# Start of the QKV projection and order of later loads in a fused attention and SwiGLU kernel

## Chip, cores and metric

The kernel runs on one core of a Trainium2 chip. The metric is the time of one execution on the device, in microseconds; lower is better.

## The reference

`x` is 2048 tokens by 576 columns, bfloat16. It is normalized once (`xn`) and goes through two branches, whose results are added to `x`:

```python
xn = _layernorm(x)                                  # (x - mean) / sqrt(var + 1e-5), by token
# A: qkv = xn @ wqkv; 32 heads of 18; each token attends to itself and to the tokens
#    2, 4, ... 14 before it (8 positions, softmax); o @ wo
# B: (silu(xn @ w_gate) * (xn @ w_up)) @ w_down      with 4608 inner columns
return x + _A_ref(xn, A_wqkv, A_wo) + _B_ref(xn, B_w_gate, B_w_up, B_w_down)
```

## The kernel before

Tokens are split into 16 row tiles ("rows" below) of 128 tokens, and four token tiles of four rows each. The order of the work is written out by hand (`tc.manual_schedule()`): each engine runs its instructions in the order in which the Python code issues them. Nearly all transfers are issued from SyncE's queue (SP), in order; each transfer takes the next of eight completion semaphores in turn, and the issue of a transfer waits until the one eight before it has landed. PSUM is a ring of eight banks (`new_ps`, `new_pt`).

**Start, row 0 and row 1** (L477 to L525). The loads at L154 to L165 bring x rows 0 to 3 one by one, the QKV weights in five slices of 128 (the last: 64) input columns, and then x rows 4 to 15 in three transfers. Slice 1 and x row 0 go over ScalarE's queue, all others over SP's. `warm_pe` (L171) runs matmuls on constants until the first data is there. Row 0 is only centred (mean taken off) before it is turned: `ln_stats(0)` takes mean and variance on VectorE by two `bn_stats` (L214) and one `bn_aggr` (L218), `ln_center` (L248) takes the mean off, first for 128 columns and then for the rest, `transp_pe` (L258) turns 128 x 128 blocks on TensorE into PSUM and `copy_pt` (L267) copies them out. Its factor 1/sqrt(var + eps) is multiplied into the products when they leave PSUM (`p_evac`, L363 to L367); `ln_apply(0)` also makes a fully normalized copy, which is turned by a transfer (`transp_dma`). All other rows are normalized fully first (`ln_stats`, `ln_sqrt`, `ln_recip`, `ln_apply`).

The products of row 0 (`p_whole`, L304) go slice by slice: four matmuls of 128 x 432, one for each group of 432 columns of q, k, v, for each slice. Row 1's five blocks are turned between them (L501 to L507): blocks 0 and 1 into the bank of the warm-up (`pt1`), block 2 into `pa`, 3 and 4 into `pb`; `pa` and `pb` held row 0's blocks. ScalarE copies out the first and the last pair, VectorE block 2. Row 1's products of slice 0 follow, then row 0's slice 3 and slice 4 (`p_row0_rest`, two pairs of 64-row halves).

**Rows 1 to 15** (L523 to L577). `p_row` multiplies one row by all weights with 64-row matmuls that run in pairs. Rows 2 to 4 are turned on TensorE inside the products of the row before (`turn`), rows 5 to 15 by transposing transfers (`transp_dma`, L291). Keys and values are stored to the ring tiles `Kr` and `Vr`, or for the later token tiles to a buffer in HBM (`kv_d`, `store`). `load_wd(7)` (L533) loads the eighth chunk of the down projection's weights, 576 KB, after row 1. The tile `wd` holds x and the normalized rows in its first seven chunks until they are used up.

**Token tiles** (L647 to L684). For each token tile nine chunks of 512 inner columns run: `g_pair` (L601) multiplies by the gate and up weights of the chunk, `g_evac` applies silu and the product. The weights of a chunk (1.15 MB, `gu`, four transfers, L182 to L185) stand in one of two slots; those of chunk n + 2 are issued when chunk n is done. In the first token tile, the remaining weights of the down projection (`load_wd`, L193) and of the output projection (`load_wo`, L190) are loaded beside: chunk `ch` issues `load_wd(ch - 1)` for 1 to 7, and chunk 5 also `load_wd(8)`. Attention for the next token tile runs on VectorE in between (a list of pieces that `dve.pump` works off), with its ring loads (`ring_load`, L389). The residual `xr` (four rows of x, two transfers of 288 KB, L672 to L674) is loaded at chunk 0 in the first token tile and at chunk 7 in the others. After chunk 8 the attention output is turned by four transfers (L659), and `d_half` (L630) multiplies by `wd` and `wo` and `d_out` (L642) adds the residual.

Of the kernel before, what the change touches and what calls it, by code (L numbers as in the profile page):

```python
# [70 lines left out]
def kernel(  # L71
# [83 lines left out]
    load_x(nc.sync, 1)  # L155
    load_w(nc.scalar, 1)
    load_w(nc.sync, 0)
    make_identity(nc, ident[:])
# [4 lines left out]
    load_x(nc.sync, 3)  # L163
    for c in range(1, 4):
        nc.sync.dma_start(xc_b[c], x_v[:, 4 * c:4 * c + 4, :])  # L165
    nc.scalar.activation(warm[:], eps_t[:], ACT.Sqrt)

    wp = ps.tile([P, 512], f32, name="warm_ps", tag="ps")
    pt1 = wp[:].bitcast(bf16)

# [35 lines left out]

    sums = {}

    def ln_half(r, k):
# [38 lines left out]
    def ln_center(r, lo=0, hi=D):  # L248
        c, j = divmod(r, 4)
        xc, xn, mv, rstd = ln[c]  # L250
        nc.vector.tensor_scalar(xn[:, j, lo:hi], xc[:, j, lo:hi], mv[:, j, 0:1], None, op0=ALU.subtract)  # L251

    def ln_center_pad(r):
        c, j = divmod(r, 4)
        xc, xn, mv, rstd = ln[c]
        nc.gpsimd.tensor_scalar(xn[:, j, D:DPAD], xc[:, j, 512:D], mv[:, j, 0:1], None, op0=ALU.subtract)

# [218 lines left out]

    warm_pe(10, 1)  # L477
    ln_open(0)
    ln_stats(0)
    ln_center_pad(0)  # L480
    ln_center(0, 0, P)
    ln_sqrt(0)
    pa, pb = new_pt(), new_pt()
# [7 lines left out]
    copy_pt(nc.scalar.copy, 0, (3, 4), pb[:, 2 * P:])  # L491
    ln_recip(0)
    ln_apply(0)
    ln_recip(1)
    ln_apply(1)

    t = [new_ps("qkv_ps") for g in range(NG)]
    p_whole(0, t, 0)
    p_whole(0, t, 1)
    p_whole(0, t, 2, (0, 1))  # L500
    transp_pe(1, (0, 1), pt1)  # L501
    transp_pe(1, (2,), pa)
    copy_pt(nc.scalar.copy, 1, (0, 1), pt1)
    copy_pt(nc.vector.tensor_copy, 1, (2,), pa)
    p_whole(0, t, 2, (2, 3))
    transp_pe(1, (3, 4), pb)
    copy_pt(nc.scalar.copy, 1, (3, 4), pb)  # L507
    u = [None] * NG
# [4 lines left out]
    p_row0_rest(t)  # L513
    ln_stats(2)
    ln_sqrt(2)
    normalize(2)
# [14 lines left out]
    for ring in (Kr, Vr):  # L531
        nc.sync.dma_start(ring[0:1, 0:HALO, :], wz[0:1, :].unsqueeze(1).to_broadcast([1, HALO, D]))
    load_wd(7)  # L533

# [112 lines left out]
    for tt in range(NTT):  # L647
        for ch in range(NCH):
            it = tt * NCH + ch
            for p in range(2):  # L650
                g_pair(tt, ch, p)
                for j in (2 * p, 2 * p + 1):
                    g_evac(ch, j)
                    if it % NCH < NCH - 1 or p == 0:
                        dve.pump(1.4)
            if ch == NCH - 1:
                dve.drain(lambda: chains[0] > tt)
                for r in range(RT * tt, RT * tt + RT):
                    nc.sync.dma_start_transpose(oT[:, :, r * P:(r + 1) * P], QOP[:, r, :])  # L659
            if it + NSLOT < NTT * NCH:  # L660
                load_gu(it + NSLOT)
            if tt == 0:
                if 1 <= ch <= 7:
                    load_wd(ch - 1)
                if ch == 5:
                    load_wd(8)
                for _ in range(3 if ch in (1, 2) else 2):
                    if wo_order:
                        load_wo(wo_order.pop(0))
                if ch == 0:  # L670
                    store(2, 3, 3)
            if ch == (7 if tt else 0):  # L672
                for i in (0, 2):
                    nc.sync.dma_start(xr[:, i:i + 2, :], x_v[:, RT * tt + i:RT * tt + i + 2, :])  # L674
            if ch == 1 and tt < NTT - 1:
                chain(tt + 1)
# [38 lines left out]
```

## Time and profile before

| | us |
|---|---|
| median of 3 runs | 503.55 (503.23 to 503.98) |
| the profiled execution's own time | 504.4 |
| its span | 502.6 |
| TensorE matmul busy | 498.1 |
| VectorE busy | 329.2 |
| ScalarE busy | 200.7 |
| start of the first product of row 0 | 5.93 |
| start of the token tiles (first `g_ps` in the chain) | 59.92 |

PE is TensorE, PEld its weight loads, DVE VectorE, ACT ScalarE, POOL GpSimd, SP SyncE; "SPq" is an issue on SP's queue. A timeline line has the start in us, the length in us, the engine, the line of the kernel, the operation, the tile it writes and reads, the shapes, the count and in brackets the idle time before it. A line of the chain has start, length and what the chain passed through. In the list of waits: who waited for whom, us in total, how often, longest.

### The profile page before, as it was taken

To read this page: it belongs to the slowest core of one execution; us is meant where nothing else is said; L and a number is where in the kernel's file an instruction comes from. 1 tells how busy PE (TensorE), PEld (TensorE's weight loads), DVE (VectorE), ACT (ScalarE), POOL (GpSimd) and SP (SyncE) were. 2 spreads that over 40 slices of the span, in tenths; PEclk is the share of its full clock that TensorE was granted. 3 is DMA by queue.
4 is the path that set the end of the run, shared out by engine and by line. 5 is a ranking of instruction groups with operands and counts; after the bars stand their busy time and mean duration, and the time that the engine had idled before them with its cause. 6 is when DMAs were issued, how large, how long until landed. Compare 5 with 4: busy or idle time off the path is not lost.

```text
span 502.6 us, 13267 instructions
## 1 busy us (share of the span) xinstructions
PE 498.1 (99%) x5795; PEld 333.8 (66%) x5795; DVE 329.2 (65%) x478; ACT 200.7 (40%) x415; POOL 2.6 (1%) x9
## 2 busy tenths in 40 slices
PE   9999999999999999999999999999999999999997
PEld 4555544455899755555999655556999555557997
DVE  6888598888999698999898139995980222221001
ACT  4756657654400155554300454558000454553000
POOL 2000000000000000000000000000000000000000
PEclk9999999999999999999999999999999999999999
DMA  8999989789721036536730054455600335453100
GB/s 316 216 205 230 313 281 312 223 263 305 190 94 61 25 122 206 176 116 222 152 91 37 27 187 139 145 188 154 139 25 14 103 108 181 152 180 38 29 14 25
DMA packets 77186, 75.42 MB, mean 150 GB/s; under 512 B 22708, under 2 KB 72528, under 8 KB 77128
## 3 DMA queue, kind: packets, MB, share of 16 engines
q1 hardware_dynamic: 76840, 73.98, 50.3%
q8 instruction: 45, 0.74, 0.6%
q10 hardware_dynamic: 288, 0.59, 0.3%
q14 instruction: 13, 0.11, 0.1%
HBM read 58.76 MB, written 5.90 MB: 129 GB/s over the span
## 4 chain that ended last, share of the span: by engine, by line
PE 96%; DMA 3%; DVE 0%; ACT 0%; SPq 0%; issue 0%
PE g_ps L601 54%; PE d_ps L630 32%; PE qkv_ps L301 10%; DMA gu<-in_B_w_up_dram 2%; DMA xnT<-wd 1%; DMA wd<-in_A_x_dram 1%; DVE stats L214 0%; DVE wd L251 0%; PE pt L262 0%; ACT ot L644 0%; SPq L182 0%; PE pt L283 0%; DVE mv L218 0%; PE warm_ps L262 0%
## 5 line engine op out<-in xcount | busy, mean ns | idle before, releaser
L601 PE MATMUL g_ps<-xnT,gu 64*128 64x512 bf16 x2592 | 281.5, 376 | 0.3 <-DMA gu<-in_B_w_up_dram 0.3
L601 PEld LDWEIGHTS <-gu 64*128 64x128 bf16 x2592 | 144.8, 94 | 135.6 <-DMA gu<-in_B_w_up_dram 0.8
L630 PE MATMUL d_ps<-wd,hT 64*128 64x288 bf16 x2304 | 152.5, 283 | 0.0
L612 ACT ACTIVATE sg<-g_ps 128x512 bf16<-128x512 f32 x144 | 87.3, 606 | 157.5 <-PE g_ps L601 157.5
L630 PEld LDWEIGHTS <-hT 64*128 64x128 bf16 x2304 | 144.6, 94 | 0.5
L614 DVE TENSOR_TENSOR hT<-sg,uc 128x512 bf16<-128x512 bf16 x144 | 60.0, 418 | 94.3 <-ACT uc L613 94.2
L613 ACT CAST uc<-g_ps 128x512 bf16<-128x512 f32 x144 | 85.2, 592 | 0.0
L414 DVE TENSOR_REDUCE PP<-PP 128x64 f32<-128x1152 bf16 x64 | 84.9, 1345 | 0.4
L301 PE MATMUL qkv_ps<-hT,xnT 64*128 64x432 bf16 (+1 forms) x536 | 50.2, 343 | 0.2 <-DMA xnT<-wd 0.2
L409 DVE TENSOR_TENSOR PP<-QO,Kr 128x2304 bf16<-128x2304 bf16 (+1 forms) x35 | 43.5, 1249 | 7.8 <-DMA Kr<-hT 7.5
L642 DVE TENSOR_TENSOR ot<-d_ps,xr 128x288 bf16<-128x288 f32 x30 | 12.3, 450 | 51.1 <-PE d_ps L630 51.0
L441 DVE TENSOR_TENSOR PP<-Vr,A 128x2304 bf16<-128x2304 bf16 (+1 forms) x35 | 43.2, 1250 | 0.4
L301 PEld LDWEIGHTS <-xnT 64*128 64x128 bf16 (+1 forms) x536 | 25.8, 94 | 22.9 <-DMA xnT<-wd 0.6
L446 DVE TENSOR_TENSOR PP<-PP 128x2304 bf16<-128x2304 bf16 x24 | 32.5, 1353 | 0.3
L630 PE MATMUL d_ps<-wo,xnT 64*128 64x288 bf16 x288 | 29.1, 283 | 0.0
L612 ACT ACT_TABLE_LOAD x5 | 6.4, 1283 | 47.2 <-PE g_ps L601 47.2
L630 PEld LDWEIGHTS <-xnT 64*128 64x128 bf16 x288 | 21.2, 94 | 0.0
L363 ACT CAST hT<-qkv_ps 128x288 bf16<-128x288 f32 (+2 forms) x58 | 21.0, 423 | 0.3 <-DMA kv_d<-hT 0.3
L434 ACT ACTIVATE PP<-PP 128x1024 f32<-128x1024 f32 x4 | 4.2, 1057 | 31.3 <-DVE PP L430 31.2
L644 ACT CAST ot<-d_ps 128x288 bf16<-128x288 f32 x1 | 0.4, 399 | 38.7 <-PE d_ps L630 38.7
L363 ACT CAST QO<-qkv_ps 128x432 bf16<-128x432 f32 (+1 forms) x30 | 12.2, 405 | 7.9 <-PE qkv_ps L301 7.9
L214 DVE BATCH_NORM_STATS2 stats<-wd 128x6 f32<-128x288 bf16 x32 | 12.9, 443 | 3.0 <-DMA wd<-in_A_x_dram 2.8
(53 smaller groups left out, 90.8 us busy)
## 6 DMA issues: line engine op xcount, KB each, us to landing
gu<-in_B_w_gate_dram SPq DMA_DIRECT2D x36, 512.0 KB, 3.8
gu<-in_B_w_up_dram SPq DMA_DIRECT2D x36, 512.0 KB, 5.3
wd<-in_B_w_down_dram SPq DMA_DIRECT2D x9, 576.0 KB, 6.1
kv_d<-hT SPq DMA_DIRECT2D x5, 576.0 KB, 5.9
gu<-in_B_w_gate_dram SPq DMA_DIRECT2D x36, 64.0 KB, 4.8
gu<-in_B_w_up_dram SPq DMA_DIRECT2D x36, 64.0 KB, 4.4
xr<-in_A_x_dram SPq DMA_DIRECT2D x8, 288.0 KB, 5.0
out_dram<-ot SPq DMA_DIRECT2D x16, 144.0 KB, 1.8
```

Source lines behind the costliest of these rows:

```text
L214: nc.vector.bn_stats(sums[r][:, k, :], xc[:, j, k * HALF:(k + 1) * HALF])
L301: return nc.tensor.matmul(t[g][:, 0:G], xT_of(r)[rows, kt, :], w_at(g, kt, rows), start=start, stop=stop)
L363: (nc.vector.tensor_copy if n in dve else nc.scalar.copy)(*parts[n])
L409: nc.vector.tensor_tensor(prod[:, a:b], QO[:, RT * tt + a:RT * tt + b, :], Kr[:, s:s + b - a, :], op=ALU.mult)
L414: nc.vector.tensor_reduce(L[:, w, rs], prod[:, rs].rearrange("p r (h d) -> p r h d", d=DH), axis=AX.X, op=ALU.add)
L441: nc.vector.tensor_tensor(dst[:, a:b], Vr[:, s:s + b - a, :].rearrange("p r (d h) -> p r d h", h=H), A[:, w, a:b].unsqueeze(2).to_broadcas ...
L446: nc.vector.tensor_tensor(dst, acc, pv, op=ALU.add)
L601: mm = nc.tensor.matmul(ring_ps[j][b][:], gu[rows, slot, k, fc], xnT[rows, kt, tok], start=(swap == 0 and kt == 0), stop=(swap == 1 and kt ...
L612: nc.scalar.activation(sg[:], t[0][:], ACT.Silu)
L613: nc.scalar.copy(uc[:], t[1][:])
L614: nc.vector.tensor_tensor(hT[:, ch * FC + j, :], sg[:], uc[:], op=ALU.mult)
L630: mm = nc.tensor.matmul(t[sub][h][:, 0:HALF], a[rows], w[rows, h * HALF:(h + 1) * HALF], start=(swap == 0 and n == 0), stop=(swap == 1 and ...
```

## The change

- The QKV weight slices 0 and 1 are each loaded in two halves of 864 columns; ScalarE's queue takes the upper halves, SP's the lower.
- x rows 8 to 15 come in one transfer.
- Row 0's mean is not taken from `bn_stats`: `ln_mean0` sums x/576 over columns 0 to 287 on ScalarE and over 288 to 575 on VectorE, each with an accumulator output, and `ln_center` takes both sums off. The statistics of row 0 (still wanted for its variance and its normalized copy) move between and behind those of row 1; its square root, reciprocal and apply move behind row 1's copies and row 2's statistics.
- Row 1's blocks 0 to 2 are turned after slice 1's products instead of half way through slice 2's, blocks 3 and 4 after three of slice 2's four; all go to the bank `pb` and are copied by ScalarE.
- One warm-up matmul less.
- `load_wd(7)` leaves the start: chunk 3 issues `load_wd(8)` and chunk 4 `load_wd(7)` beside their own; chunk 5 has one again.
- The store of the last values goes in two parts, not three. The residual `xr` is loaded after chunk 8's output transposes, in all token tiles.

```diff
-    load_w(nc.scalar, 1)
-    load_w(nc.sync, 0)
+    for kt in range(2):
+        for eng, cols in ((nc.scalar, slice(2 * G, 4 * G)), (nc.sync, slice(0, 2 * G))):
+            eng.dma_start(wqkv[:, kt, cols], A_wqkv[kt * P:(kt + 1) * P, cols])
...
-    for c in range(1, 4):
-        nc.sync.dma_start(xc_b[c], x_v[:, 4 * c:4 * c + 4, :])
+    nc.sync.dma_start(xc_b[1], x_v[:, 4:8, :])
+    nc.sync.dma_start(wdf[:, 2 * XC:4 * XC].rearrange("p (r d) -> p r d", d=D), x_v[:, 8:16, :])
...
-    pt1 = wp[:].bitcast(bf16)
...
+    part = const.tile([P, 2], f32, name="part")
+
+    def ln_mean0():
+        xc = ln[0][0]
+        nc.scalar.activation(PP[:, 1, 0:HALF], xc[:, 0, 0:HALF], ACT.Copy, scale=1.0 / D, accum_out=part[:, 0:1])
+        nc.vector.tensor_scalar(PP[:, 1, HALF:D], xc[:, 0, HALF:D], 1.0 / D, None,
+                                op0=ALU.mult, op1=ALU.add, accum_out=part[:, 1:2])
...
-        nc.vector.tensor_scalar(xn[:, j, lo:hi], xc[:, j, lo:hi], mv[:, j, 0:1], None, op0=ALU.subtract)
+        nc.vector.tensor_scalar(xn[:, j, lo:hi], xc[:, j, lo:hi], part[:, 0:1], part[:, 1:2],
+                                op0=ALU.subtract, op1=ALU.subtract)
...
-    warm_pe(10, 1)
+    warm_pe(9, 1)
     ln_open(0)
-    ln_stats(0)
+    ln_mean0()
     ln_center_pad(0)
     ln_center(0, 0, P)
-    ln_sqrt(0)
...
     copy_pt(nc.scalar.copy, 0, (3, 4), pb[:, 2 * P:])
-    ln_recip(0)
-    ln_apply(0)
+    ln_half(0, 0)
     ln_recip(1)
     ln_apply(1)
+    ln_half(0, 1)
+    ln_aggr(0)
...
     p_whole(0, t, 1)
-    p_whole(0, t, 2, (0, 1))
-    transp_pe(1, (0, 1), pt1)
-    transp_pe(1, (2,), pa)
-    copy_pt(nc.scalar.copy, 1, (0, 1), pt1)
-    copy_pt(nc.vector.tensor_copy, 1, (2,), pa)
-    p_whole(0, t, 2, (2, 3))
-    transp_pe(1, (3, 4), pb)
-    copy_pt(nc.scalar.copy, 1, (3, 4), pb)
+    transp_pe(1, (0, 1, 2), pb)
+    copy_pt(nc.scalar.copy, 1, (0,), pb)
+    copy_pt(nc.scalar.copy, 1, (1, 2), pb[:, P:])
+    p_whole(0, t, 2, (0, 1, 2))
+    transp_pe(1, (3, 4), pb[:, 3 * P:])
+    copy_pt(nc.scalar.copy, 1, (3, 4), pb[:, 3 * P:])
+    p_whole(0, t, 2, (3,))
+    ln_sqrt(0)
+    ln_stats(2)
+    ln_sqrt(2)
+    ln_recip(0)
+    ln_apply(0)
...
     p_row0_rest(t)
-    ln_stats(2)
-    ln_sqrt(2)
     normalize(2)
...
-    load_wd(7)
...
                 for r in range(RT * tt, RT * tt + RT):
                     nc.sync.dma_start_transpose(oT[:, :, r * P:(r + 1) * P], QOP[:, r, :])
+                for i in (0, 2):
+                    nc.sync.dma_start(xr[:, i:i + 2, :], x_v[:, RT * tt + i:RT * tt + i + 2, :])
...
-                if ch == 5:
-                    load_wd(8)
+                if ch in (3, 4):
+                    load_wd(11 - ch)
...
                 if ch == 0:
-                    store(2, 3, 3)
-            if ch == (7 if tt else 0):
-                for i in (0, 2):
-                    nc.sync.dma_start(xr[:, i:i + 2, :], x_v[:, RT * tt + i:RT * tt + i + 2, :])
+                    store(2, 3, 2)
```

More of the change, by code (lines that the diff above doesn't have):

```diff
@@ L255, in ln_center_pad @@
         xc, xn, mv, rstd = ln[c]
-        nc.gpsimd.tensor_scalar(xn[:, j, D:DPAD], xc[:, j, 512:D], mv[:, j, 0:1], None, op0=ALU.subtract)
+        nc.gpsimd.tensor_scalar(xn[:, j, D:DPAD], xc[:, j, 512:D], part[:, 0:1], part[:, 1:2],
+                                op0=ALU.subtract, op1=ALU.subtract)
     def transp_pe(r, kts, pt):
```

## The prediction

> **What bounds the kernel now.** I read the share of busy time first, then what TensorE waited for, then the chain that ended last, and then the timeline of the places that these name. The page and TensorE's list of waits:
>
> ```profile
> span 502.6 us, 13267 instructions
> PE 498.1 (99%) x5795; PEld 333.8 (66%) x5795; DVE 329.2 (65%) x478; ACT 200.7 (40%) x415; POOL 2.6 (1%) x9
> ...
> PE warm_ps L174 <- PEq L699: 0.8, 1, 0.8
> PE g_ps L601 <- DMA gu<-in_B_w_up_dram: 0.3, 1, 0.3
> PE qkv_ps L301 <- DMA xnT<-wd: 0.2, 1, 0.2
> ```
>
> TensorE is never without work but for its start and two waits on transfers. Only what shortens the start, or these two waits, or adds a new wait can move the time. The chain places them:
>
> ```profile
> 0.72 3.19 DMA wd<-in_A_x_dram
> ...
> 3.93 0.83 DVE stats L214 x2
> ...
> 18.97 4.60 DMA xnT<-wd
> 23.57 0.05 issue
> 23.62 36.31 PE qkv_ps L301 x396
> ...
> 83.71 7.80 DMA gu<-in_B_w_up_dram
> 91.51 0.05 issue
> 91.56 39.12 PE g_ps L601 x359
> ```
>
> The ends of matmuls are modelled, so I take waits from start to start. At 23.62 a pair comes 0.50 us after the one before it, where 0.18 is usual: row 5's wait costs 0.32. At 91.56 it is 0.71 for 0.21: chunk 4's wait costs 0.50. From 91.56 to the end nothing waits. The timeline of the start:
>
> ```profile
> 5.03 0.56 DVE L251 TENSOR_SCALAR wd<-wd,mv 128x128 bf16<-128x128 bf16 x2
> 5.93 2.00 PE L301 MATMUL qkv_ps<-hT,PP 128*128 128x432 bf16 x10
> 7.16 0.43 DVE L240 TENSOR_SCALAR wd<-wd,mv,rstd 128x576 bf16<-128x576 bf16 x1
> 7.76 0.28 PE L262 MATMUL warm_ps<-ident,wd 128*128 128x128 bf16 x2
> 8.08 0.37 ACT L268 COPY xnT<-warm_ps 128x256 bf16<-128x256 bf16 x1 [0.92 <-PE warm_ps L262]
> 9.24 1.36 PE L301 MATMUL qkv_ps<-hT,PP 128*128 128x432 bf16 x8
> ```
>
> Row 0's centring starts at 5.03, its first product 0.90 later, slice 3's at 9.24, and slice 4's at 10.07 (four products of 0.18 and a 0.1 switch to half rows). Two windows (us, busy time by engine, clock, share of the DMA engines, GB/s):
>
> ```profile
> 3.00:5.50 2.50, 2.40 (x8) 0.68 (x5) 1.50 (x5) 0.44 (x2) 0.40 (x1) 1.00 1.01 401
> 98.00:99.50 1.50, 1.50 (x16) 0.79 (x14) 1.50 (x3) 0.66 (x2) 0.00 (x0) 1.00 0.10 25
> ```
>
> The first window is full: the weights come no faster. By issue and time to landing, slice 3 lands at 2.59 + 6.4 = 9.0 and is used at 9.24; the last of slice 4 lands at 3.92 + 5.9 = 9.8 and its product runs at 10.07. So whatever row 0 gains, TensorE can come forward by some 0.25 us only.
>
> **The change, part by part.**
>
> **Row 0's mean.** Removed ahead of the centring: two statistics and an aggregate, 3.93 to 5.03 = 1.10 us. Added: one half sum on ScalarE and one on VectorE, side by side, and a hand-over. No row shows a summing operation. The nearest are ScalarE's 288-wide ACTIVATE at 0.50 and VectorE's L251 (0.25 for 128 columns, 0.40 for 448, so 0.33 for 288); VectorE took up a ScalarE result 0.04 after its end (9.65 to 9.69). Low bound 0.33 + 0.04, high bound 0.83, the two statistics that go. I take ScalarE's row and 0.1 for hand-over and read-out: 0.60, so centring at 4.53, 0.50 sooner. The Trainium skill's page "VectorE: DVE Perf Modes", section "Two Vector instructions with no wait between them", says that an operation that writes its accumulator out is two instructions, the second a read of it; no row here shows one, and by it (an estimate, with the 0.11 to 0.16 of a one-column RECIPROCAL) VectorE's half is 0.44 to 0.49, still under ScalarE's, so the sum stays.
>
> **Row 1.** From its start the centring needs 2.56 us until row 1 is normalized (7.59). Behind it now: two statistics of row 1, the aggregate, one half statistic of row 0 (0.37 from start to start) in place of a reciprocal and an apply (0.49), reciprocal, apply: 2.5, so 7.03, transposes at 7.1. TensorE ends slice 1's products at 4.53 + 0.90 + 8 x 0.183 = 6.9 and waits 0.2. Then three transposes and three products of slice 2. The next two transposes write the same bank `pb` that ScalarE reads, and so wait for its copies: third transpose's end 0.33 after 7.1, hand-over 0.04, copies 0.27 + 0.37, so 8.1, where the products were done at 7.8: another 0.3 wait, which three banks spared the kernel before. Two transposes 0.11, a product 0.18, four products of row 1 0.73: slice 3 at 9.15 against 9.24. Slice 2 (1.64 + 5.6 = 7.2) is in time.
>
> **Slices in halves.** Two more issues, on two queues, and 0.88 MB in rows half as long. Bounds: nothing, by the window 3.00 to 5.50; or the 267 GB/s of 8.00 to 9.40, where slice 4's equally short rows come, against 401: 0.88 MB in 3.3 us for 2.2, 1.1 more, on all weights behind. I take 0.1: same tensor, 128 partitions, as in the first row. Slice 3's issue now waits for x row 0 (3.9), the last of slice 4 for a half of slice 0, x row 3 and those behind likewise; the engines are full until 7.5 and beyond, and first bytes come 1 to 1.5 us after an issue, so this is covered; without that cover it would cost those 1.5 us. Slice 3 at 9.1, slice 4 at 9.9. Start: 10.07 becomes 10.0, gain **0.05**, bounds +0.25 (all weights as before) and -0.9. One warm-up matmul less (0.43 us) goes from ahead of a wait and is worth nothing. Row 0's statistics, square root and apply move behind row 1's and are wanted only at the evacuation at 10.46; VectorE's row 2 is done by 10.6 for TensorE's 12.09.
>
> **Down projection chunk 7 later.** Its 576 KB fill 19 to 22 us, just ahead of row 5's transpose: issued 18.97 (VectorE releases it at 18.94), landed 4.6 later; the next took 2.6, the longest one after 4.3. Without it: 21.6 to 23.3, before the 23.3 at which TensorE wants it. Gain between 0 and 0.32, I take **0.32**: both ends of the landing do it. Late next is row 6's transpose, landed 24.5 for a use at 26.6.
>
> **Residual later, store in two parts.** Chunk 0 sheds two loads of 288 KB (issues 73.05, 73.99) and one store issue from SP. The loads are out of the engines by 77, where chunk 3's weights begin: in the second microsecond after their issue the engines moved 134 GB/s, part still the residual, and 167 for chunk 2's. About 0.1 MB late, 0.3 us at 366 GB/s, handed on by full engines through a down projection chunk, the K ring load and chunk 4's weights. Bounds 0 (they caught up) and 0.50 (the whole wait); I take **0.30**. The residual now stands behind the four output transposes on SP (130.8 to 136.0): two issues, 1.2 us, ahead of weights that are wanted at 178; landed about 142, for the first L642 at 145.7. Later tiles likewise. The two issues merged into one for x rows 8 to 15 free SP 0.4 us: nothing.
>
> **Chunks 7 and 8 at chunks 3 and 4.** Each adds 576 KB behind that chunk's weights, 2.0 us of full engines (112 to 116 us hold two). After chunk 3's the engines are idle from 98.2 to 100.5: it fits. After chunk 4's only 107.8 to 108.5 is idle: chunk 7's weights come up to 1.3 late, and they land at 109.0 + 4.4 = 113.4 for a use at 115.1: 1.7 in hand. Two slices in one chunk stood before at chunk 5, with no wait behind. **0**, bounds 0 and +1.6 (below).
>
> Sum: -0.05 - 0.32 - 0.30 = -0.67. The profiled execution itself took 504.4 us (1.8 around the span), so it would become 503.7; it lies 0.85 above the median, and the same sum on the median gives **502.9**.
>
> **Rivals.**
> - *All of it is gained.* No loss on the halves, centring before 4.4: 0.25 + 0.32 + 0.50 = 1.07, **502.5**. For it: slice 4 has 0.25 in hand. Against: the copies that hold `pb`.
> - *The late chunks starve the gate and up weights* (slower). Place: chunks 6 and 7. If each 2.0 us is paid in full, chunk 6's weights (landed 106.6, wanted 107.3) come 1.3 late and chunk 7's 0.3: +1.6 - 0.67 = +0.95, **504.5**. It decides from 0.7 us of delay at chunk 6. For it: at 91.5 just such a queue made TensorE wait. Against: the idle engines of 98.00 to 99.50.
> - *The start gets slower.* Halves at 267 GB/s: 0.9 later, less 0.62: **503.8**.
> - *The clock rises late.* The warm-up's 512-column matmuls stand 0.43 apart and later 432-column ones 0.18, so the speed doubles, between 4.98 and 5.65. If the shorter warm-up let it stay low for as long again as it did (4.2 us from the first matmul at 0.76, so to 9.2), the eight products of slices 0 and 1 take 2.9, row 1's transposes and slice 2 run low in part, and slice 4 starts near 11.3: +1.24 - 0.62, **504.2**. The Trainium skill's page "TensorE: Matmul & The Clock Gate", Part 1, has the clock rise after a busy window of about 3.4 us that runs free of the kernel; by that rule this could happen in some executions; the trace has one rise and no late one.
> - *The two waits are there under the profiler only* (0.85 above the median): nothing but the start counts, **503.5**.
>
> **Numbers.** Forecast 0.50; all gained 0.25; starved 0.12; slower start or late clock 0.08; nothing 0.05. A measurement tells about 0.2%, 1.0 us, from no change. Faster by more: the second case and a little of the first, 0.28; slower: the third and part of the fourth, 0.16; same 0.56. The range 502.1 to 504.4 takes in the gained case with 0.4 to spare and the starved case but for its end; the likeliest case alone spans 502.5 to 503.3.
>
> **What would show it.** Right: centring near 4.5; two short TensorE waits, at the transposes and at the copies of row 1; slice 3 near 9.1; no wait before row 5's products; chunk 4's wait 0.2 or less; none at chunks 6 and 7. Wrong: a TensorE wait on `hT` weights near 6 to 10 us, on `gu` at 106 or 114 us, or 0.36 us between 432-column products after 5.3 us.

## The result and the profile after

The changed kernel takes 504.61 us (median of 22 runs, 503.41 to 505.89), the kernel before on the same chip 503.55 us (22 runs, 503.23 to 504.50). The ratio is 1.0020, 95% interval 1.0014 to 1.0026: slower by about 1.1 us. 502.9 was forecast, with 504.4 as the end of the range. What strikes at once is the spread: 2.5 us, where the kernel before has 1.3 on this chip. (In the five sets of runs below the kernel before spreads by 2.0 to 2.8 us, so a spread as such is not the changed kernel's alone.)

The profiled execution of the changed kernel was its slowest, 505.89 us (1.8 around the span of 504.1). First the page's lines and TensorE's list of waits:

```profile
span 504.1 us, 13269 instructions
PE 497.0 (99%) x5794; PEld 282.6 (56%) x5794; DVE 329.3 (65%) x479; ACT 201.2 (40%) x418; POOL 2.8 (1%) x9
...
PE qkv_ps L310 <- DMA hT<-in_A_wqkv_dram: 2.6, 2, 1.4
PE warm_ps L174 <- PEq L708: 0.8, 1, 0.8
PE pt L271 <- DVE wd L258: 0.4, 1, 0.4
```

The two waits of before (row 5's transpose, chunk 4's weights) are gone. In their place stand 2.6 us of waiting for QKV weights, the first of the prediction's signs of being wrong. The chain that ended last (start, length, what it passed through) no longer begins with x row 0 and has no transfer behind 9.5 us:

```profile
1.17 0.46 ACTq L158
...
1.66 7.81 DMA hT<-in_A_wqkv_dram
9.47 0.04 issue
9.51 0.53 PE qkv_ps L310 x2
...
21.68 40.52 PE qkv_ps L310 x444
62.20 69.93 PE g_ps L611 x648
132.13 39.69 PE d_ps L640 x648
```

The transfer is the upper half of slice 1, on ScalarE's queue: issued at 1.66, landed at 9.47. From 21.68 to the end TensorE never waits. The first gate and up product starts at 62.20 in this chain (59.92 before): 2.3 lost, all of it ahead of the token tiles. The timeline of the start:

```profile
3.90 0.33 SPq L149 DMA_DIRECT2D hT<-in_A_wqkv_dram  x1
3.90 0.44 ACT L212 ACTIVATE PP<-wd 128x288 bf16<-128x288 bf16 x1 [0.26 <-DMA wd<-in_A_x_dram]
3.90 0.45 DVE L213 TENSOR_SCALAR_CACHE_REDUCE PP<-wd 128x288 bf16<-128x288 bf16 x1 [2.70 <-DMA wd<-in_A_x_dram]
4.25 0.18 ACT L212 ACTIVATION_READ_ACCUMULATOR PP<-wd 128x1 f32 x1
4.28 0.08 DVE L213 DVE_READ_ACCUMULATOR PP<-wd 128x1 f32 x1
4.49 0.62 DVE L258 TENSOR_SCALAR wd<-wd,part 128x128 bf16<-128x128 bf16 x2
5.45 0.91 PE L310 MATMUL qkv_ps<-hT,PP 128*128 128x432 bf16 x4
7.72 0.52 PE L310 MATMUL qkv_ps<-hT,PP 128*128 128x432 bf16 x2 [1.37 <-DMA hT<-in_A_wqkv_dram]
9.48 0.33 SPq L165 DMA_DIRECT2D wd<-in_A_x_dram  x1
9.51 0.53 PE L310 MATMUL qkv_ps<-hT,PP 128*128 128x432 bf16 x2 [1.27 <-DMA hT<-in_A_wqkv_dram]
```

The centring starts at 4.49 and the first product at 5.45, both earlier than before. But slice 1's lower half lets its first two products go only at 7.72 and the upper half the other two only at 9.51. Slice 3's issue on SP stands at 3.90, where x row 0 landed, instead of 2.59. The first product of slice 4, which the prediction put at 10.0, starts at 12.68 in this trace. I call this moment "slice 4's start" below.

Last, the two windows that were shown of before (busy time by engine, clock, DMA share, GB/s):

```profile
3.00:5.50 2.50, 2.03 (x12) 0.80 (x11) 1.47 (x6) 1.43 (x5) 0.66 (x1) 1.00 1.04 374
98.00:99.50 1.50, 1.50 (x18) 0.68 (x14) 1.50 (x3) 0.40 (x1) 0.00 (x0) 1.00 1.08 319
```

The DMA engines are as full at the start as before (374 for 401 GB/s in this execution), and the idle stretch at 98 is now used. No wait follows from it.

### The profile page after: what moved, and what is told of

It is laid out like the page before. It is cut to its first block, busy times and chain, and to the rows that moved or that the text cites. A ratio compares the mean times of both kernels' runs of the same rounds, so it can differ in the third digit from the quotient of the medians.

```text
span 504.1 us, 13269 instructions
## 1 busy us (share of the span) xinstructions
PE 497.0 (99%) x5794; PEld 282.6 (56%) x5794; DVE 329.3 (65%) x479; ACT 201.2 (40%) x418; POOL 2.8 (1%) x9
## 4 chain that ended last, share of the span: by engine, by line
PE 97%; DMA 2%; ACTq 0%; ACT 0%; DVE 0%; issue 0%
PE g_ps L611 55%; PE d_ps L640 32%; PE qkv_ps L310 10%; DMA hT<-in_A_wqkv_dram 2%; ACT xnT L277 0%; ACTq L158 0%; PE pt L271 0%; DVE ot L654 0%; PE pt L292 0%; ACTq L145 0%
## 5 line engine op out<-in xcount | busy, mean ns | idle before, releaser
L611 PEld LDWEIGHTS <-gu 64*128 64x128 bf16 x2592 | 126.1, 94 | 152.9
L640 PE MATMUL d_ps<-wd,hT 64*128 64x288 bf16 x2304 | 146.3, 283 | 0.0
L640 PEld LDWEIGHTS <-hT 64*128 64x128 bf16 x2304 | 112.0, 94 | 29.8
L640 PE MATMUL d_ps<-wo,xnT 64*128 64x288 bf16 x288 | 22.9, 283 | 0.0
L640 PEld LDWEIGHTS <-xnT 64*128 64x128 bf16 x288 | 14.0, 94 | 3.6
```

Of the source, the lines that this page charges most:

```text
L611: mm = nc.tensor.matmul(ring_ps[j][b][:], gu[rows, slot, k, fc], xnT[rows, kt, tok], start=(swap == 0 and kt == 0), stop=(swap == 1 and kt ...
L640: mm = nc.tensor.matmul(t[sub][h][:, 0:HALF], a[rows], w[rows, h * HALF:(h + 1) * HALF], start=(swap == 0 and n == 0), stop=(swap == 1 and ...
```

## The experiments

All kernels below compute the same. "Start" is slice 4's start in the one trace of each. Ratios are to the kernel before on the same chip, and weigh its long runs too; kernels of different groups ran on different chips, where the kernel before had medians of 503.95 (e1 to e4; 503.27 to 506.04), 503.77 (e5 to e8), 503.80 (e9, e10, a1, a2), 503.59 (a3 to a5, e11) and 503.68 (e12, e13). So ratios, and not medians, are compared across groups.

| kernel | what it has | median us (range, runs) | ratio, 95% interval | start |
|---|---|---|---|---|
| the kernel before | | 503.55 (503.23 to 504.50, 22) | 1 | 10.07 |
| changed | all | 504.61 (503.41 to 505.89, 22) | 1.0020 [1.0014, 1.0026] | 12.68 |
| e1_whole | all but the halves | 504.41 (503.98 to 504.70, 11) | 1.0005 [0.9995, 1.0015] | 10.30 |
| e2_halves | the halves alone | 504.81 (503.75 to 506.26, 12) | 1.0020 [1.0008, 1.0031] | 10.33 |
| e3_late | the late loads alone | 503.31 (503.18 to 504.29, 11) | 0.9986 [0.9978, 0.9995] | 10.01 |
| e4_mean | sums and row 1's order alone | 505.06 (504.54 to 505.57, 11) | 1.0019 [1.0010, 1.0027] | 10.29 |
| e5_shift | e1 and one more ScalarE instruction | 503.57 (503.29 to 503.83, 11) | 0.9991 [0.9982, 1.0000] | 10.27 |
| e6_sameq | e3 and halves, each slice on its old queue | 503.83 (503.53 to 504.32, 11) | 0.9999 [0.9990, 1.0008] | 10.44 |
| e7_all_halves | e3 and slices 0 to 3 in halves | 504.49 (504.13 to 506.32, 11) | 1.0014 [1.0001, 1.0028] | 11.05 |
| e8_mean_only | e3 and the sums | 503.53 (503.22 to 503.83, 11) | 0.9989 [0.9981, 0.9998] | 10.26 |
| e9_two_queues | e3 and the halves | 503.88 (503.58 to 505.07, 11) | 1.0002 [0.9993, 1.0011] | 10.32 |
| e10_no_lane | e9, slice 3 ahead of x row 2 | 503.95 (503.75 to 504.86, 11) | 1.0004 [0.9995, 1.0014] | 10.06 |
| a1_look, a2_look | changed | 504.43, 503.64 | | 11.26, 10.47 |
| a3_timed | changed | 504.37 (503.64 to 504.89, 11) | 1.0011 [1.0002, 1.0020] | 11.53 |
| a4_look, a5_look | changed | 503.64, 504.00 | | 10.44, 10.64 |
| e11_w3_first | changed, slice 3 ahead of x row 2 | 504.88 (504.05 to 507.02, 11) | 1.0029 [1.0017, 1.0041] | 11.12 |
| e12_sums_halves | e8 and the halves | 503.60 (503.23 to 505.13, 12) | 0.9999 [0.9989, 1.0009] | 11.01 |
| e13_row1_halves | e9 and row 1's order | 504.24 (503.72 to 505.69, 12) | 1.0009 [0.9999, 1.0020] | 10.87 |

### The change taken apart: e1 to e4

My theory after the first trace was that the halves alone lose the time, and that the sums and the late loads gain what was forecast. The rival was that the sums and the new order of row 1 lose at the start.

e1_whole, the changed kernel with whole slices:

```diff
-    for kt in range(2):
-        for eng, cols in ((nc.scalar, slice(2 * G, 4 * G)), (nc.sync, slice(0, 2 * G))):
-            eng.dma_start(wqkv[:, kt, cols], A_wqkv[kt * P:(kt + 1) * P, cols])
+    load_w(nc.scalar, 1)
+    load_w(nc.sync, 0)
```

> The changed kernel with slices 0 and 1 whole again (slice 1 on ScalarE's queue, slice 0 on SP's). Theory 'halves': the half slices on ScalarE's queue land late and cost the start some 2 us; without them the start gives back that loss and the two waits stay gone: 502.7 to 503.1, faster than before by 0.5 to 0.8. Rival 'row 0's mean and row 1's order': the halves only happened to be hit by one stalled packet in the profiled execution; then this kernel stays near 504.6. Rival 'later loads': also 504.6.

e2_halves is the kernel before with the reverse of this edit.

> The kernel before with only the half slices. Theory 'halves': slower by 1 to 2 us, 504.5 to 505.5, with TensorE waiting on QKV weights between 6 and 10 us. Rivals 'row 0's mean' and 'later loads': 503.4 to 503.7, as before.

e3_late is the kernel before with the loads of the late part of the change and nothing else:

```diff
-    load_wd(7)
...
                     nc.sync.dma_start_transpose(oT[:, :, r * P:(r + 1) * P], QOP[:, r, :])
+                for i in (0, 2):
+                    nc.sync.dma_start(xr[:, i:i + 2, :], x_v[:, RT * tt + i:RT * tt + i + 2, :])
...
-                if ch == 5:
-                    load_wd(8)
+                if ch in (3, 4):
+                    load_wd(11 - ch)
...
-                    store(2, 3, 3)
-            if ch == (7 if tt else 0):
-                for i in (0, 2):
-                    nc.sync.dma_start(xr[:, i:i + 2, :], x_v[:, RT * tt + i:RT * tt + i + 2, :])
+                    store(2, 3, 2)
```

> The kernel before with only the later loads (down projection chunks 7 and 8 at chunks 4 and 3, the residual after chunk 8, the store in two parts). If both waits (0.32 before row 5, 0.50 before chunk 4) are there without the profiler: 502.7 to 503.2. If they are there under the profiler only: 503.5. Rival 'later loads' (they starve chunks 6 or 7): 504.5.

e4_mean is e1_whole with the late loads and the x transfers of before, so that row 0's sums, the moved statistics, row 1's order and the ninth warm-up are left.

> The kernel before with only row 0's mean from sums, row 1's new order and one warm-up matmul less; whole slices, old loads. By the step of the prediction the start gains 0.05 to 0.1: 503.4 to 503.6. Rival 'row 0's mean and row 1's order': 504.5 or more, with new TensorE waits at the transposes of row 1.

Measured: e3_late 503.31, e2_halves 504.81, but e1_whole 504.41 and e4_mean 505.06. The late loads gain 0.14% and the halves lose 0.20%, as the theory had it; e2_halves' trace is of its fastest execution (503.75) and does not show the loss. The sums and row 1's order, however, seemed to lose 0.19%. In e3_late's trace TensorE waits for no transfer at all:

```profile
PE warm_ps L174 <- PEq L697: 0.8, 1, 0.8
PE pt L262 <- DVE wd L251: 0.2, 1, 0.2
```

For e1_whole and e4_mean the theory missed, and the start does not explain it: slice 4 starts at 10.30 and 10.29, 0.2 later than before, and not 1 us. The rest of e1_whole's loss lies at the other end. From the last product's start to the end of the span e1_whole took 4.56 and e4_mean 4.03, where all others took 3.3 to 3.7. (e4_mean, with the loads of before, also has row 5's wait in its trace: 0.53 from start to start, at 24.04.) The transfers from 499 to 502 us in e1_whole (packets, MB and share by queue; the last line has the us from issue to landing):

```profile
q1 hardware_dynamic: 144, 0.15, 14.0%
q14 instruction: 1, 0.01, 0.7%
issues: line engine op xcount, KB each, median us to landing
out_dram<-ot SPq DMA_DIRECT2D x1, 144.0 KB, 2.8
```

One packet of program code (8 KB) lies in the last output store, and the store lands 2.8 us after its issue instead of 1.7. In the traces such a packet follows ScalarE's 574th recorded instruction (issues, semaphores and drains counted) by 1.0 to 2.0 us. The kernel before has 574 of them, so there it comes after the end. e1_whole and e4_mean have 578, and it falls onto the last store. The changed kernel has 579, with ScalarE's second weight issue; there the 574th runs at 478.7, the packet goes out at 479.8, 24 us ahead of the end, and the last store lands in 1.7 us.

### Moving the code transfer: e5

```diff
     nc.scalar.activation(warm[:], eps_t[:], ACT.Sqrt)
+    nc.scalar.activation(warm[:], eps_t[:], ACT.Sqrt)
```

> The changed kernel with slices 0 and 1 whole, and one small ScalarE instruction more at the start (the activation on one column that loads the square root's table, a second time), so that ScalarE runs 579 recorded instructions instead of 578; it computes the same. Theory A (a transfer of program code spoils the end): in e1_whole and e4_mean one 8 KB transfer of instructions lies in the last output store, issued after ScalarE's 574th recorded instruction, and the store lands 2.75 and 2.34 us after its issue instead of 1.73. With one instruction more that transfer goes out some 20 us before the end, the tail behind the last product goes back from 4.56 to 3.4, and the time falls by about 1.0 us: 503.3 to 503.6 where e1_whole had 504.4 (before: 503.95). Theory B (the sums and the new order of row 1 cost 1 us at the start): no change, 504.3 to 504.6. One instruction cannot cost less than nothing at the start, so a fall of 0.7 or more speaks for A alone.

503.57 us, ratio 0.9991 for 1.0005, from an instruction that does nothing new. The same window of e5_shift:

```profile
q1 hardware_dynamic: 144, 0.15, 13.8%
issues: line engine op xcount, KB each, median us to landing
out_dram<-ot SPq DMA_DIRECT2D x1, 144.0 KB, 1.7
```

The code packet is gone and the store lands in 1.7. Theory A holds. The loss of e1_whole was an artefact of where ScalarE's program ends, and no cost of the sums. e4_mean was not run again with an instruction more; in its trace the tail has 0.6 us of this, and row 5's wait is most of the rest. Of the changed kernel it takes nothing away, because that kernel did not have it. So the whole change without the halves has a ratio of 0.9991 (503.57), and with them 1.0020 (504.61) and, on another chip, 1.0011 (a3_timed).

### What the halves cost: e6, e7, e9, e10

All are built on e3_late, so that no later wait hides anything. e6_sameq keeps both halves of a slice on one queue:

```diff
-    load_w(nc.scalar, 1)
-    load_w(nc.sync, 0)
+    for h in (slice(2 * G, 4 * G), slice(0, 2 * G)):
+        nc.scalar.dma_start(wqkv[:, 1, h], A_wqkv[P:2 * P, h])
+        nc.sync.dma_start(wqkv[:, 0, h], A_wqkv[0:P, h])
```

> The late loads alone (e3_late: 503.31, ratio 0.9986) and slices 0 and 1 in column halves, but each slice on the queue that it had: both halves of slice 0 on SP, both of slice 1 on ScalarE's. Theory P (packet length: on a DMA engine that has fallen behind, packets of the two queues alternate, so 1,728-byte packets move half as many bytes as the 3,456-byte ones of slice 2 beside them): slice 1 is late in some executions as with the halves over two queues, 504.0 to 504.6, spread of 1.5 us or more. Theory Q (a slice spread over both queues waits for the later of the two): no loss, 503.2 to 503.6, spread as in e3_late.

e7_all_halves loads slices 0 to 3 in this way over both queues, with two ScalarE instructions more as in e5_shift:

```diff
+    def load_halves(kt):
+        for eng, cols in ((nc.scalar, slice(2 * G, 4 * G)), (nc.sync, slice(0, 2 * G))):
+            eng.dma_start(wqkv[:, kt, cols], A_wqkv[kt * P:(kt + 1) * P, cols])
```

> The late loads alone and slices 0 to 3 all in column halves over the two queues, so that packets of one length alternate until slice 4 (two small ScalarE instructions more at the start keep ScalarE's transfer of code out of the last store). Theory P: slice 1 loses nothing to slice 2, 503.2 to 503.6. Theory Q: every slice now waits for the later of two queues, 504.2 to 505.2. A third way: short rows move slower for all weights (267 GB/s instead of 401 for 1.77 MB, 2.2 us): 505 or more, and the trace shows the DMA engines busy until past 10 us.

e8_mean_only, which ran with these, is e5_shift with row 1's old order, ten warm-ups and one more repeat of the small activation:

```diff
-    warm_pe(9, 1)
+    warm_pe(10, 1)
...
-    transp_pe(1, (0, 1, 2), pb)
...
+    p_whole(0, t, 2, (0, 1))
+    transp_pe(1, (0, 1), pt1)
+    transp_pe(1, (2,), pa)
...
+    p_whole(0, t, 2, (2, 3))
+    transp_pe(1, (3, 4), pb)
```

> The late loads and row 0's mean by the two sums, with row 1 turned in the order and into the three banks of before and ten warm-up matmuls; slices whole; ScalarE again at 579 recorded instructions. If the two waits on bank pb (0.25 us in the traces of e1_whole and e4_mean, at row 1's last two transposes) are all that the new order costs, this is 0.1 to 0.3 faster than e5_shift: 503.1 to 503.3, slice 4 at 9.9 to 10.05. If row 0's earlier centring is worth nothing (TensorE's clock still low at the first products, or slice 0 not there), it equals e3_late: 503.2 to 503.5.

It came out at 503.53, as e5_shift (503.57) and, by the ratios, as e3_late. The 0.25 us wait on bank `pb` is gone from its trace, and slice 4 starts at 10.26 all the same: its first three products ran slow. So nothing measurable is gained or lost by the sums.

e6_sameq came out between the theories, at 503.83 with a spread of 0.8. Its trace shows neither of them: slice 3's issue waits for x row 0 (3.93), slice 3 lands at 9.57, and its products start at 9.61, 0.16 late. e7_all_halves cannot judge: its ScalarE held the issue of slice 3's half until 4.19 behind x row 0's landing, its table load came behind that, and so the copies of row 0 were late:

```profile
PE qkv_ps L307 <- ACT PP L274: 0.4, 1, 0.4
PE pt L268 <- DVE wd L257: 0.3, 1, 0.3
```

That made a third theory, L: the two transfers more use up two of the eight completion semaphores. e9_two_queues is e3_late with the halves exactly as in the changed kernel. e10_no_lane makes slice 3 the eighth transfer again:

```diff
-    load_x(nc.sync, 2)
     load_w(nc.sync, 3)
+    load_x(nc.sync, 2)
```

> The late loads alone and slices 0 and 1 in column halves as in the changed kernel: lower halves on SP, upper ones on ScalarE's queue. Beside e6_sameq (both halves of a slice on one queue: 503.83, 503.53 to 504.32) only the assignment to queues differs. Theory Q (a slice spread over two queues waits for the later one): 504.2 to 505.0, with a spread of 1.5 us or more, and the start of slice 4 at 10.4 or later. Theory L (the two transfers more push slice 3's issue behind the landing of x row 0, as the eight completion semaphores come round: 3.93 instead of 2.60 in e6_sameq, slice 3 landed 9.57, wanted 9.46): the same as e6_sameq, 503.6 to 504.1.

> e9_two_queues with x row 2's transfer issued behind slice 3's instead of ahead of it, so that slice 3 is the eighth transfer and its issue waits for no landing. Theory L: slice 3 issued at 2.6, landed by 9.1, no wait before its products, slice 4's start at 10.0 to 10.3, and the time that of e3_late, 0.9980 to 0.9990 of before. Theory Q: as e9_two_queues within 0.3 us.

e9_two_queues had 503.88 beside e6_sameq's 503.83. The queue assignment as such costs nothing, and theory Q falls. The timeline of e9_two_queues:

```profile
4.00 0.33 SPq L149 DMA_DIRECT2D hT<-in_A_wqkv_dram  x1
...
9.50 1.47 PE L302 MATMUL qkv_ps<-hT,PP 128*128 128x432 bf16 x8
```

and of e10_no_lane:

```profile
2.14 0.91 SPq L149 DMA_DIRECT2D hT<-in_A_wqkv_dram  x2
...
9.24 1.47 PE L302 MATMUL qkv_ps<-hT,PP 128*128 128x432 bf16 x8
...
9.36 0.82 DVE L215 BATCH_NORM_STATS2 stats<-wd 128x6 f32<-128x288 bf16 x2 [1.00 <-DMA wd<-in_A_x_dram]
...
13.74 0.54 PE L302 MATMUL qkv_ps<-hT,xnT 64*128 64x432 bf16 x4 [0.32 <-ACT QO L364]
```

With the order changed, slice 3 is issued straight behind slice 2 (two issues from 2.14 on), lands at 8.58, and slice 4 starts at 10.06 as before. But x row 2 now pays: its statistics wait 1.00 us, and TensorE waits at 13.74 (0.49 from start to start beyond the usual 0.18). The time stays at 503.95. So theory L is right that the issue waits, and its forecast of the time missed (0.9980 to 0.9990, measured 1.0004): moving the wait only moves the victim.

How much halves and late issue cost at the landing is not the same in each execution. Slice 2 is issued at 1.63 to 1.68 with whole slices and at 2.10 to 2.15 with halves, as one more issue stands ahead of it on SP. It landed at 7.11 to 7.19 in the six traces with whole slices, and at 7.19 to 7.58 in the six with slices 0 and 1 in halves and no late packet (see below): 0 to 0.4 later, short rows and later issue together. Slice 3 landed at 8.72 to 9.19 with whole slices. Its issue waited for x row 0 in five of the six with halves: there it landed at 9.46 to 9.60 in four, and at 8.80 in e2_halves, which has the same start as e9_two_queues. Issue to landing of slice 3, in e2_halves and in e9_two_queues (issued at 3.92 and 4.00):

```profile
hT<-in_A_wqkv_dram SPq DMA_DIRECT2D x1, 432.0 KB, 4.9
```

```profile
hT<-in_A_wqkv_dram SPq DMA_DIRECT2D x1, 432.0 KB, 5.5
```

So a late issue can stay without cost, as the prediction had it, and in four of these five traces slice 3 was later all the same.

### Where the changed kernel's spread comes from: a1 to a5, e11

Short rows and the wait of theory L ("lane wait") make 503.6 to 503.9, and not 504.61. So five more executions of the changed kernel were traced, one of them with times beside it, and one with e10_no_lane's edit (e11_w3_first).

> The changed kernel once more, for its trace. If the 2.6 us of waits on slices 0 and 1 in the first trace are what the kernel commonly pays, slice 4 starts at 11 us or later here too, with a wait before the third product of slice 1. If that trace was a rare one and the common cost is the lane wait of theory L, slice 4 starts at 10.3 to 10.6, and the wait stands before slice 3.

> The same once more: as for a1_look. From the first product of row 0's slice 4 to the end nothing should differ from the other traces with late loads: 49.36 us to the token tiles, 438.61 from there to the last product's start.

> The changed kernel once more, timed, with a trace. Theory S (one stalled packet of slice 1 in most executions, at no cost in the others): times spread from 503.5 to 505.9 with a median of 504.2 to 504.8; in the trace, the start of slice 4 less 10.45 (the lane wait alone, as in a2_look) equals what the trace's stalled packet made late. Theory L alone (the lane wait, and the first trace was a rare one): median 503.5 to 503.9, spread under 1 us.

> The changed kernel, for its trace. Theory S: either a packet of slice 1 over 0.6 us near 5.6 us and slice 4 at 11 or later, or none and slice 4 at 10.4 to 10.6.

> As a4_look. A slice 4 start of 11 or later without a packet over 0.6 us near 5.6 us speaks against theory S.

> The changed kernel with x row 2 issued behind slice 3. Theory L: slice 3 issued at 2.6 and landed by 9.0, slice 4's start near 9.7 to 10.0 where nothing stalls; row 2's statistics are late instead (x row 2 landed at 9.3 in e10_no_lane, where TensorE waited 0.5 at 13.7), so the median falls by 0 to 0.4 only. Theory S: the stalls stay, spread of 1.5 us or more, median within 0.4 of a3_timed.

In the six traces of the changed kernel slice 4 starts at 10.44, 10.47, 10.64, 11.26, 11.53 and 12.68, and the execution takes 503.64, 503.64, 504.00, 504.43, 504.74 and 505.89. The difference is 493.2 each time (493.17 to 493.36). The whole spread is made in the first 13 us. A good execution, a2_look, has a chain that begins with x row 0 and passes through no weight transfer at the start:

```profile
0.73 3.30 DMA wd<-in_A_x_dram
...
5.31 0.61 PE pt L271 x4
5.92 1.72 PE qkv_ps L310 x8
```

A poor one, a3_timed, hangs on slice 3, which was issued when x row 0 had landed and took 6.76 us where a2_look's took 5.6 (4.05 to 9.60):

```profile
3.90 6.76 DMA hT<-in_A_wqkv_dram
10.66 0.04 issue
10.70 3.02 PE qkv_ps L310 x26
```

What is late is the tail of slice 1. ScalarE's queue carries nothing behind it. In the window from 5.75 to 8.60 us that queue (q10) should be empty. In e3_late it is but for one small packet, in the first trace of the changed kernel nine packets are left, in a3_timed four:

```profile
q10 hardware_dynamic: 1, 0.00, 0.0%
```

```profile
q10 hardware_dynamic: 9, 0.01, 1.3%
```

```profile
q10 hardware_dynamic: 4, 0.01, 1.6%
```

The last of them went out at 8.36 and 7.12 us, and slices 2 and 3 behind them on SP's queue were late too. Theory S, one stalled packet, explains the first trace (1.63 us on one packet at 5.53) and a1_look (0.76 at 5.76), but not a3_timed, where no packet from 4 to 8.6 us took over 0.56 us. a4_look came as it said (10.44, no long packet); a5_look had a packet of 0.65 us and started slice 4 at 10.64, which is neither of the two cases. Theory S falls as put. Something near it stands: from 4 to 8.6 us the longest packet took 0.51 to 1.63 us in each of the seven traces with late packets, and 0.18 to 0.56 in the other twelve (e7_all_halves left out). Why a packet takes so long is not shown. e11_w3_first kept the late packets (last one at 6.89) and added the wait on row 2: 504.88.

### Sums or row order beside the halves: e12, e13

e12_sums_halves is e8_mean_only with the halves; e13_row1_halves is e9_two_queues with the changed kernel's order of row 1. In both the number of repeats of the small activation is set so that ScalarE has 579 instructions (one fewer than in e8_mean_only, three more than in e9_two_queues).

```diff
 (e12_sums_halves, to e8_mean_only)
-    load_w(nc.scalar, 1)
-    load_w(nc.sync, 0)
+    for kt in range(2):
+        for eng, cols in ((nc.scalar, slice(2 * G, 4 * G)), (nc.sync, slice(0, 2 * G))):
+            eng.dma_start(wqkv[:, kt, cols], A_wqkv[kt * P:(kt + 1) * P, cols])
 (e13_row1_halves, to e9_two_queues)
-    transp_pe(1, (0, 1), pt1)
-    transp_pe(1, (2,), pa)
...
+    transp_pe(1, (0, 1, 2), pb)
...
+    transp_pe(1, (3, 4), pb[:, 3 * P:])
```

> e8_mean_only (late loads, row 0's mean by sums, row 1's old order; 503.53, 503.22 to 503.83) with slices 0 and 1 in halves over two queues; ScalarE again at 579 recorded instructions. If the halves cost what they cost without the sums (the lane wait, e9_two_queues 503.88): 503.7 to 504.1, spread near 1 us. If sums and halves together bring the late packets: median 504.3 to 504.8, spread 1.3 us or more, and in the trace, when late, the last packets of ScalarE's queue after 6.5 us.

> e9_two_queues (late loads and halves, no sums; 503.88, 503.58 to 505.07) with row 1 turned in the new order into bank pb; ScalarE at 579 recorded instructions. If the late packets come with the sums: 503.8 to 504.2 (0.25 us at most for bank pb). If they come with the new order of row 1: 504.3 or more. If neither this nor e12_sums_halves shows them, they come with the chip or at random, and their cause stays open.

Late packets stand in both traces (last ones at 6.50 and 6.35), so neither the sums nor the order of row 1 is needed for them. The halves are, as far as the traces go: counting those in which the last packet of ScalarE's queue went out after 5.9 us, it is 7 of 13 with slices 0 and 1 in halves (e7_all_halves, with more on that queue, left out), and none of 6 with whole slices, whose last one went out at 5.1 to 5.6. Whether the halves are enough, the traces do not show: the four with halves and neither sums nor the new order (e2, e6, e9, e10, ScalarE at 575 instructions) have none, the nine others (579) have the seven. How often it strikes differs: with row 1's new order 34 of 56 runs (changed, a3, e11, e13) took more than 504.3 us, with the old order 6 of 45 (e6, e9, e10, e12), with whole slices and the late loads none of 33 (e3, e5, e8). With the loads of before, whose waits come and go, it is 9 of 12 with halves and the old order (e2) and 28 of 155 of the kernel before, so these are not compared. On one chip, e12 and e13 have 503.60 and 504.24: the first lies under its lower case, though its traced execution (504.82) has late packets, the second between its cases. With whole slices the order makes no difference (e5_shift 503.57, e8_mean_only 503.53). Since these ran on different chips, and since I know no way by which TensorE's order could delay a packet, this stays open, and with it why a half slice's last packets are held up at all.

## Why the prediction was wrong

**The late loads: the mechanism right, but taken off the wrong time.** Forecast -0.32 for row 5 and -0.30 for chunk 4. e3_late has -0.14% (0.05 to 0.22), 0.7 us on its chip. From slice 4's start to the first gate and up product it takes 49.36 us in its trace for 49.69 before, and from there to the last product's start 438.61 for 439.50: row 5's 0.32, chunk 4's 0.50 and some 0.4 more. But the two waits do not come in each execution with the loads of before. TensorE's whole list of waits in e2_halves, which has these loads, and the end of row 5's wait in e4_mean, the other such trace:

```profile
PE warm_ps L175 <- PEq L700: 0.8, 1, 0.8
```

```profile
24.04 0.48 PEld L309 LDWEIGHTS <-xnT 64*128 64x128 bf16 x8 [0.79 <-DMA xnT<-wd]
```

e2_halves has neither wait (49.36 and 438.61, as with the late loads), e4_mean has row 5's and not chunk 4's (49.90 and 438.60). The prediction read both waits in an execution that lay 0.85 above the median and took them off the median. With slice 4's start at 10.07 and nothing waiting behind it the kernel before would take 10.07 + 493.2 = 503.3 (an estimate), and its fastest run in each of the six sets of runs took 503.18 to 503.41. So of the median of 503.55 these waits can have some 0.3 and not 0.62, and no run of any kernel was under 503.18: 502.9 was out of reach. What the late loads remove is long executions: none of e3_late's 11 runs is over 504.3, and 11 of the kernel before's 35 on that chip are, up to 506.04. What the longest of these paid no trace shows; it is more than the 1.2 us of the first profile. The rival of starved chunks found next to no support: of 17 traces with the late loads one (e12_sums_halves) shows a gap before a product of chunk 7, 0.21 us, and is 0.7 us longer than the others from the first gate and up product to the last product.

**The sums and row 1's order: the cost right, the gain nothing.** The centring came at 4.49 (4.53 forecast). The summing operations took 0.44 and 0.45; with their read-outs of 0.18 and 0.08 and the hand-over that makes 0.59 from 3.90 to 4.49, and 0.60 was taken. The Trainium skill's page "VectorE: DVE Perf Modes", section "Two Vector instructions with no wait between them", has the accumulator's read as a second instruction; the traces agree, with 0.08 us for it, and show the same on ScalarE with 0.18. What the earlier centring is worth with whole slices is nothing: e8_mean_only (0.9989) against e3_late (0.9986). Three things are in its way. Slice 3 lands near 9, as the prediction said. A product that starts before the clock is up runs slow: in e8_mean_only the first products start at 5.79, 6.10 and 6.46, then 0.22 and 0.18 apart, so that 0.3 is lost. And slice 0, which the prediction took to be there at 4.53 + 0.90 = 5.43, landed at 6.00, 5.71 and 5.74 in e1_whole, e5_shift and e8_mean_only, and the first product started 0.04 to 0.05 later. e1_whole's trace lists the wait:

```profile
PE qkv_ps L309 <- DMA hT<-in_A_wqkv_dram: 0.7, 1, 0.7
```

With halves the first product starts at 5.29 to 5.71 in the six traces of the changed kernel: this is what the halves buy, and the later slices take it back. The two short waits at row 1 were one, of 0.25 us, in each of e1_whole, e4_mean and e5_shift: the copies that hold bank `pb`.

**The halves: the step that failed.** "Slice 3's issue now waits for x row 0 (3.9) [...] the engines are full until 7.5 and beyond, and first bytes come 1 to 1.5 us after an issue, so this is covered [...] Slice 3 at 9.1". The issue waited as said (3.68 to 4.05 in the six traces), the engines were full, and yet slice 3 landed at 9.58 at best. That full engines would hide the late issue was taken for sure; of the five traces with halves, late issue and no late packets the forecast of 9.1 held in one (8.80), and in four slice 3 came 0.4 to 0.5 after it (9.46 to 9.60). How much of that is the issue and how much the shorter rows, priced at 0.1, is not separated. With slice 3 wanted at 9.24 and landing near 9.0 there was no room for it. Where slice 3 was the last to come, slice 4 starts 0.87 after its landing (9.58 and 10.44, 9.60 and 10.47, 9.78 and 10.64, 10.39 and 11.26, 10.66 and 11.53), which is why any delay shows in full. Against whole slices this part is small, because e5_shift starts slice 4 at 10.27 anyway: a2_look took 503.64 and e5_shift's traced execution 503.60.

The larger part had no term at all. The halves were priced by rate (0.1, bounds 0 and 1.1), as if a transfer's landing followed from the mean rate. What the kernel pays is the last packets of slice 1, which went out after 5.9 us, up to 8.4, in five of the seven traces of the changed kernel and e11_w3_first, where whole slices end at 5.1 to 5.6. By the sum above a median of 504.61 means a slice 4 start near 11.4: 1.0 beyond the 10.45 of the executions without late packets. The rival "the start gets slower" had the place and the sign, but its mechanism, short rows at 267 GB/s and 0.9 us for it, is there at less than half of that size, 0 to 0.4 us at slice 2. Why the last packets are late stays open.

So of the 1.7 us between forecast and median some 1.0 is late packets, 0.4 slice 4's start at 10.45 for 10.0 (e5_shift, with whole slices, had 10.27), and 0.3 the waits that the median did not have (an estimate from the constant of 493.2).

**The rivals of the clock and of waits under the profiler only.** The clock was not late in the sense meant: in all traces it is up by about 6.6 us, with nine warm-ups or ten. The sign named for it, 0.36 us between products after 5.3, is there for one product in a2_look (5.71) and two in a3_timed (5.57 and 5.93). The two waits are there outside the first profile, as e3_late's gain makes likely, but only in some executions; profiled ones without them exist, as e2_halves shows.

So even without the halves the sum of -0.67 (0.13%) is not reached for sure: e5_shift and e8_mean_only have -0.09% and -0.11%, with intervals up to 0 and -0.02%, and medians 0.2 us under the kernel before's. e3_late has the best ratio of all that was run. The late loads alone are faster than both kernels by more than the measurement is uncertain.

## What to carry to other kernels

Price an added transfer by what it pushes back, not by its bytes: list the order of issues, count round the eight completion semaphores, and find the transfer whose issue now waits for a landing. Where a product waits for the last packet of a transfer, the mean rate says little, and one trace does not show whether a landing is firm: the traces of six executions did, and one constant among them (time less slice 4's start) showed that all the spread had one place. The same holds for a wait that is to be removed: if the profiled execution lies above the median, ask whether the median has the wait at all. And when a part of a change seems to cost 1 us at a place where it has no work, look at the end of the trace for a transfer of code before believing it.

## What the runs showed of the hardware

- A transfer of 8 KB of program code that falls into the last output store delayed its landing from 1.7 to 2.3 and 2.8 us. One more ScalarE instruction at the start of its program moved it away, worth 0.7 to 0.8 us.
- The time at which 432-column products come to 0.18 us apart, or 512-column warm-ups leave 0.43, varied from 3.4 to 6.6 us from execution to execution, with either number of warm-ups. The Trainium skill's page "TensorE: Matmul & The Clock Gate", Part 1, has the clock rise after a busy window of about 3.4 us that runs free of the kernel; the spread of 3.2 us agrees with a free window, while the earliest rise came 2.6 us after the first matmul (0.76), sooner than 3.4.
- The last packets of ScalarE's queue, of 1,728 bytes, went out 0.4 to 2.7 us later than the latest of whole rows, beside the other queue's longer ones, in 7 of 13 traces; the last whole rows of 3,456 bytes went out by 5.6 in all 6. Its cause is open.
